# A fused recurrence and mixer kernel: SyncE's loads in another order, and the whole hand-held plan of engines, orders and banks replaced

## The chip, the cores and the metric

The kernel runs on one core of one Trainium2 chip. The core has a matrix engine (TensorE, PE in the profile; its weight loads are PEld), a vector engine (VectorE, DVE), a scalar engine with function tables (ScalarE, ACT), a general engine (GpSimd, POOL) and a queue engine (SyncE, SP) that here only issues transfers. Each engine takes its instructions strictly in the order in which the program gives them and waits on semaphores for results of the others. The metric is the time of one execution on the device in microseconds (us); lower is better. Several runs give a median.

## The reference: what is computed

Two stages follow each other, for batch B = 4, H = 8 heads, S = 768 tokens and D = 40 numbers per head (DM = H x D = 320). The first is a recurrence over tokens with a 40 x 40 state per batch and head:

```python
for t in range(S):
    y[:, :, t] = np.einsum('bhd,bhde->bhe', rt, state)
    Sa = np.einsum('bhde,bhe->bhd', state, at)
    state_decay = state * wt[:, :, None, :] - np.einsum('bhd,bhe->bhde', Sa, bt)
    state = state_decay + np.einsum('bhd,bhe->bhde', vt, kt)
```

The second is a mixer over the result x (heads laid side by side, 768 x 320 per batch), with two 768 x 768 matrices over tokens and two 320 x 320 matrices over channels:

```python
theta = x @ w_theta
zr, zi = x * cos(theta), x * sin(theta)
u = x + w_tok_r @ zr + w_tok_i @ zi
out = u + np.maximum(u @ w_ch, 0.0)
```

## The kernel before

**Tiles.** The recurrence is computed in chunks of 128 tokens: 6 chunks per batch, 24 tiles in all, numbered 0 to 23. Tile i needs six loads of 160 KB: w, k, b, a, v and r. For r, and for v of tiles 0 to 7 (called o there), two tiles are loaded together as two "runs" of 160 KB. The raw tiles stand in a few rotating buffers (`raw_w`, `raw_kb` four each, `raw_a` five, `raw_v` six halves, `raw_r` two pairs), so a load must also wait until the tile that had its buffer has been used up.

**Work of one tile**, by the names that the text uses (line numbers of the kernel before):

- ACT takes the logarithm of w (`lw`, L445). PE sums it along the tokens (`cs`, L458 to L464), ACT exponentiates the sums (`ex` L469, `we` L479 or L487).
- Products scale k, b and a (`kb`, `ah`; L428 on DVE or L429 on POOL). v and r are cast to bf16 (L434 on ACT, L435 on POOL).
- PE transposes kb, ah, v, r (L391, for runs L538, for the way back L557) into PSUM, and DVE (L397) or ACT (L394, for r L546) copies the result out. Such copies out of PSUM are called evacuations here.
- PE forms four score matrices of 128 x 1024 (L569): psi, phi, lamv and, later, lamu. Each must be masked to a triangle. There are two variants: DVE multiplies by a mask while it evacuates (L578), or ACT evacuates with a sign (L580) and POOL then clears one triangle in place (an affine select, L582; called a select below).
- PE then works through the state: `x0` (L610, L616), `nx` evacuated (L622 ACT, L623 DVE), `nu` (L629, evacuated at L633 or L635), the new state `gt` (L652, evacuated at L663 and L667, or L671) and its transpose `gd` (L679, evacuated at L684), the transposed nu (L391), scores lamu (`slu`), and the tile's result y (L793 to L802), which DVE multiplies out to x (L809).

**Mixer.** For two tiles at a time PE transposes x (L711), multiplies by w_theta (L763, L773), and ACT copies theta out (L828). After the last tile of a batch ACT takes sine and cosine (L850; these and the logarithm and exponential need different function tables, hence table loads at L850 and L1024). POOL or DVE forms zr and zi (L864, L865). For each of the six rows of tokens PE accumulates 12 matmuls of 320 columns (`row`, L881), DVE adds x (L887), PE transposes (L711) and multiplies by w_ch (L763, L773, L752), DVE adds the rectified product (L917, L905) and a transfer stores 160 KB (L920, L909). Late in the run eleven transposes go through the transfer engines instead (L698).

**What sets the order.** The kernel records 1,602 operations in a plan (`Plan`, L153), each with its engine, the data it reads and writes and its predecessors. Nothing is scheduled when the program is built: `Plan.order` (L186 to L199) takes the order from three tables that stand in the file.

- `ORDER` (L26) is a permutation of all operations. The program is emitted in it, and so it is each engine's own order and the order of SyncE's queue.
- `PICK` (L138) names the operations that use their other variant, that is the other engine. For a score, the mask on ACT and its select on POOL are two operations that are picked together.
- `HOMES` (L122) gives each PSUM result its bank, in order of its first use.

`WARM` (L145) adds 49 filler matmuls ahead of five early operations. The instructions of an engine are in-order, so an operation that waits holds up whatever stands behind it in `ORDER` on its engine.

The emission loop reads:

```python
for o in plan.order():
    ...
    if o.fn is not None:
        o.fn()
```

Of the kernel before, what the change touches and what calls it, by code (L numbers as in the profile page):

```python
# [26 lines left out]
    0, 7, 3, 6, 1, 2, 20, 8, 21, 23, 24, 4, 27, 9, 32, 30, 5, 22, 31, 33, 12, 25, 26, 34, 11,  # L27
    28, 10, 69, 35, 36, 29, 70, 37, 18, 47, 44, 40, 19, 48, 72, 45, 38, 41, 71, 49, 73, 39, 46,
    98, 119, 76, 99, 58, 14, 42, 100, 74, 57, 15, 13, 120, 122, 101, 50, 121, 79, 75, 51, 123,
    53, 106, 102, 107, 131, 108, 80, 52, 16, 77, 109, 132, 125, 78, 43, 103, 81, 17, 110, 134,  # L30
    126, 111, 133, 82, 56, 84, 137, 54, 104, 124, 138, 112, 129, 83, 85, 87, 130, 88, 127, 55,
    156, 86, 128, 59, 157, 89, 146, 184, 143, 90, 147, 105, 158, 61, 97, 60, 139, 187, 159,
    135, 62, 144, 148, 164, 96, 188, 160, 165, 191, 140, 93, 136, 145, 161, 166, 141, 91, 185,
    167, 213, 186, 92, 194, 214, 149, 189, 142, 162, 168, 150, 215, 163, 169, 190, 216, 195,
    152, 221, 170, 234, 151, 246, 192, 222, 235, 193, 237, 217, 95, 236, 202, 238, 218, 94,
    196, 203, 197, 63, 241, 155, 247, 171, 267, 248, 219, 239, 199, 198, 172, 220, 223, 205,
    249, 200, 240, 271, 64, 244, 272, 242, 299, 245, 201, 154, 273, 224, 243, 300, 173, 301,
    261, 206, 254, 274, 302, 225, 174, 262, 303, 279, 153, 175, 258, 306, 176, 255, 212, 259,
    263, 280, 250, 177, 204, 281, 256, 211, 275, 496, 282, 260, 320, 226, 251, 305, 257, 208,
    252, 276, 264, 283, 253, 317, 207, 227, 349, 327, 265, 277, 497, 328, 304, 309, 278, 329,  # L40
    498, 284, 266, 310, 270, 499, 330, 350, 285, 307, 351, 268, 318, 286, 354, 308, 269, 331,
    352, 500, 311, 361, 332, 319, 287, 314, 353, 312, 209, 336, 333, 539, 362, 210, 337, 289,
    356, 288, 315, 363, 313, 322, 290, 364, 338, 355, 291, 387, 325, 292, 339, 316, 365, 540,
    388, 359, 366, 389, 541, 357, 360, 340, 390, 341, 382, 358, 391, 321, 116, 503, 113, 501,
    542, 412, 373, 181, 342, 334, 376, 374, 502, 392, 367, 411, 326, 504, 377, 375, 506, 335,
    393, 368, 505, 323, 178, 369, 545, 524, 394, 378, 370, 507, 517, 525, 413, 508, 372, 526,
    384, 371, 509, 395, 416, 396, 527, 532, 417, 528, 397, 510, 511, 514, 529, 544, 117, 595,
    512, 572, 533, 415, 383, 530, 118, 398, 573, 515, 596, 513, 554, 385, 399, 534, 531, 574,
    418, 597, 401, 535, 400, 516, 575, 414, 402, 543, 379, 324, 404, 114, 567, 598, 536, 403,
    546, 548, 115, 380, 581, 642, 576, 582, 555, 601, 549, 577, 381, 583, 599, 66, 386, 550,  # L50
    584, 537, 557, 568, 600, 551, 182, 522, 558, 602, 183, 585, 586, 538, 619, 578, 561, 587,
    419, 179, 518, 559, 547, 604, 519, 556, 427, 180, 428, 421, 429, 605, 560, 420, 606, 520,
    423, 552, 607, 626, 553, 562, 434, 422, 627, 564, 435, 425, 436, 565, 563, 643, 628, 424,
    437, 644, 610, 566, 629, 426, 613, 645, 603, 588, 611, 630, 231, 523, 571, 521, 589, 438,
    430, 570, 698, 635, 631, 646, 612, 439, 431, 636, 632, 440, 608, 745, 432, 614, 699, 647,
    609, 746, 700, 675, 648, 747, 637, 433, 615, 676, 616, 701, 293, 569, 633, 677, 748, 634,
    651, 649, 638, 678, 590, 652, 684, 296, 579, 685, 679, 617, 639, 228, 620, 621, 580, 653,
    706, 657, 591, 654, 680, 592, 618, 686, 650, 593, 661, 703, 687, 594, 441, 622, 711, 702,
    640, 442, 681, 712, 662, 688, 655, 658, 705, 656, 689, 659, 641, 663, 660, 682, 704, 664,
    690, 749, 667, 683, 665, 691, 68, 709, 692, 707, 67, 710, 729, 668, 65, 670, 672, 666, 708,  # L60
    694, 693, 750, 624, 695, 730, 719, 713, 697, 751, 720, 731, 696, 232, 732, 294, 233, 297,
    714, 721, 295, 733, 738, 298, 229, 734, 739, 715, 716, 230, 740, 735, 717, 754, 450, 752,
    451, 778, 755, 718, 346, 625, 452, 779, 453, 741, 343, 623, 756, 881, 780, 454, 757, 408,
    882, 781, 742, 405, 673, 671, 764, 883, 767, 765, 669, 782, 884, 444, 722, 455, 783, 443,
    768, 456, 766, 445, 784, 446, 736, 457, 885, 785, 458, 760, 737, 743, 447, 459, 753, 448,
    786, 787, 887, 744, 761, 796, 788, 769, 758, 460, 759, 789, 763, 461, 888, 762, 790, 462,
    797, 912, 463, 792, 791, 913, 793, 723, 770, 795, 892, 771, 914, 794, 674, 893, 915, 886,
    772, 802, 890, 464, 891, 803, 773, 347, 465, 916, 348, 344, 799, 917, 905, 805, 409, 345,
# [988 lines left out]
```

## Time and profile before

| what | value |
|---|---|
| median of 3 runs | 199.94 us (199.28 to 202.03) |
| the profiled execution, its own time | 199.53 us |
| its span, first to last instruction | 197.8 us |
| PE busy | 187.6 us, 3288 matmuls |
| DVE, ACT, POOL busy | 164.3, 151.7, 145.1 us |
| loads by SyncE | 29.19 MB in its queue, 75.1% of the transfer engines' time |
| all transfers | 32.75 MB, 166 GB/s on average |
| operations on DVE, ACT, POOL after the set-up | 236, 327, 185 |

Busy times are sums of the durations of instructions. The ends of matmuls are modelled and consecutive ones overlap, so a PE that is "busy" may still start matmuls at less than its best pace. A line number such as L397 may be that of a helper which many operations share; the tile written and read tells them apart. In a view of waits, a row names the engine and line that waited, the engine and line that released it, the total in us, how often, and the longest.

### The profile page before, as it was taken

To read this page: it belongs to the slowest core of one execution; us is meant where nothing else is said; L and a number is where in the kernel's file an instruction comes from. 1 tells how busy PE (TensorE), PEld (TensorE's weight loads), DVE (VectorE), ACT (ScalarE), POOL (GpSimd) and SP (SyncE) were. 2 spreads that over 40 slices of the span, in tenths; PEclk is the share of its full clock that TensorE was granted. 3 is DMA by queue.
4 is the path that set the end of the run, shared out by engine and by line. 5 is a ranking of instruction groups with operands and counts; after the bars stand their busy time and mean duration, and the time that the engine had idled before them with its cause. 6 is when DMAs were issued, how large, how long until landed. Compare 5 with 4: busy or idle time off the path is not lost.

```text
span 197.8 us, 8019 instructions
## 1 busy us (share of the span) xinstructions
PE 187.6 (95%) x3288; PEld 150.3 (76%) x3288; DVE 164.3 (83%) x261; ACT 151.7 (77%) x337; POOL 145.1 (73%) x210
## 2 busy tenths in 40 slices
PE   7888999999989999999999999999999999999992
PEld 6776787777768788878878888888887878767661
DVE  5269899999989999888887988999999988675453
ACT  3584979799889988979988598888998986575111
POOL 8267544679879999699799939769699697558100
PEclk9999999999999999999999999999999999999999
DMA  6999879989999999999998899988998274863055
GB/s 119 210 212 163 154 161 196 182 166 197 233 174 173 207 171 185 190 185 223 153 210 168 153 187 170 188 148 169 182 155 163 43 177 102 87 194 104 0 191 174
DMA packets 134644, 32.75 MB, mean 166 GB/s; under 512 B 124816, under 2 KB 134608, under 8 KB 134608
## 3 DMA queue, kind: packets, MB, share of 16 engines
q1 hardware_dynamic: 131680, 29.19, 75.1%
q0 software_dynamic: 2784, 2.97, 9.6%
q8 instruction: 25, 0.41, 0.9%
q10 hardware_dynamic: 144, 0.08, 0.1%
q14 instruction: 11, 0.09, 0.1%
HBM read 29.54 MB, written 3.93 MB: 169 GB/s over the span
## 4 chain that ended last, share of the span: by engine, by line
PE 68%; DMA 9%; ACT 8%; SPq 6%; DVE 3%; issue 3%; POOL 1%; ACTq 0%; DVEq 0%; POOLq 0%
PE ps_s L881 17%; PE ps_s L391 10%; PE ps_d L569 9%; PE ps_s L763 5%; SPq L409 4%; DMA raw_w<-in_w_dram 3%; DMA raw_kb<-in_k_dram 3%; PE ps_s L711 3%; PE ps_s L652 2%; PE ps_s L629 2%; SPq L421 2%; DMA raw_r<-in_r_dram 2%; PE ps_s L538 2%; PE ps_s L773 2%; ACT cs L850 2%
## 5 line engine op out<-in xcount | busy, mean ns | idle before, releaser
L429 POOL TENSOR_TENSOR kb<-raw_kb,ex 128x320 bf16<-128x320 f32 x46 | 36.8, 811 | 9.7 <-DMA raw_kb<-in_k_dram 3.3
L881 PE MATMUL ps_s<-zr,wtok_r 128*128 128x320 bf16 x132 | 37.6, 299 | 0.0
L881 PE MATMUL ps_s<-zi,wtok_i 128*128 128x320 bf16 x132 | 37.5, 299 | 0.0
L578 DVE TENSOR_TENSOR lamu<-ps_d,mask_p 128x1024 bf16<-128x1024 f32 x22 | 26.8, 1219 | 1.7 <-PE ps_d L569 1.6
L578 DVE TENSOR_TENSOR psi<-ps_d,mask_p 128x1024 bf16<-128x1024 f32 x22 | 26.8, 1218 | 1.6 <-PE ps_d L569 1.4
L578 DVE TENSOR_TENSOR lamv<-ps_d,mask_p 128x1024 bf16<-128x1024 f32 x17 | 20.7, 1218 | 2.6 <-PE ps_d L569 1.8
L429 POOL TENSOR_TENSOR ah<-raw_a,we 128x320 bf16<-128x320 f32 x22 | 19.0, 866 | 3.6 <-DMA raw_a<-in_a_dram 1.6
L578 DVE TENSOR_TENSOR phi<-ps_d,mask_n 128x1024 bf16<-128x1024 f32 x17 | 20.7, 1218 | 0.9 <-PE ps_d L569 0.8
L865 POOL TENSOR_TENSOR zi<-cs,xp 128x320 bf16<-128x320 f32 x21 | 16.9, 816 | 3.3 <-ACT cs L850 3.3
L881 PEld LDWEIGHTS <-wtok_r 128*128 128x128 bf16 x144 | 14.0, 97 | 4.5
L569 PE MATMUL ps_d<-aT,kbT 64*128 64x128 bf16 x384 | 17.1, 217 | 0.2
L881 PEld LDWEIGHTS <-wtok_i 128*128 128x128 bf16 x144 | 14.1, 98 | 3.5
L391 PE MATMUL ps_s<-wide,kb 128*128 128x128 bf16 x184 | 15.0, 223 | 1.0 <-POOL kb L429 0.7
L865 POOL TENSOR_TENSOR zr<-cs,xp 128x320 bf16<-128x320 f32 x19 | 15.3, 810 | 0.7 <-ACT cs L850 0.7
L667 POOL TENSOR_TENSOR gt<-sum,ex 128x320 bf16<-128x320 f32 x13 | 9.5, 733 | 8.0 <-DVE sum L663 4.8
L800 PE MATMUL ps_s<-kb,lamv 128*128 128x40 bf16 x192 | 15.0, 180 | 0.0
L802 PE MATMUL ps_s<-kb,lamu 128*128 128x40 bf16 x192 | 14.9, 179 | 0.0
L569 PEld LDWEIGHTS <-kbT 64*128 64x128 bf16 x384 | 11.8, 94 | 3.1 <-ACT kbT L394 1.0
L800 PEld LDWEIGHTS <-lamv 128*128 128x128 bf16 x192 | 13.2, 96 | 0.6
L887 DVE TENSOR_TENSOR up<-ps_s,xp 128x320 bf16<-128x320 f32 x22 | 10.7, 488 | 3.5 <-PE ps_s L881 3.1
L435 POOL CAST r<-raw_r 128x640 bf16<-128x640 f32 x12 | 8.6, 720 | 6.5 <-DMA raw_r<-in_r_dram 6.5
L445 ACT ACTIVATE lw<-raw_w 128x320 bf16<-128x320 f32 x24 | 11.4, 475 | 2.6 <-DMA raw_w<-in_w_dram 2.6
(176 smaller groups left out, 606.7 us busy)
## 6 DMA issues: line engine op xcount, KB each, us to landing
raw_w<-in_w_dram SPq DMA_DIRECT2D x24, 160.0 KB, 4.1
raw_v<-in_v_dram SPq DMA_DIRECT2D x24, 160.0 KB, 3.9
raw_a<-in_a_dram SPq DMA_DIRECT2D x24, 160.0 KB, 4.2
raw_kb<-in_k_dram SPq DMA_DIRECT2D x24, 160.0 KB, 3.7
raw_kb<-in_b_dram SPq DMA_DIRECT2D x24, 160.0 KB, 4.0
raw_r<-in_r_dram SPq DMA_DIRECT2D x24, 160.0 KB, 4.4
out_dram<-oo SPq DMA_DIRECT2D x9, 160.0 KB, 2.0
wrow_i<-in_moe_w_tok_i_dram POOLq DMA_DIRECT2D x6, 192.0 KB, 5.3
```

What stands on the lines that cost most here:

```text
L391: nc.tensor.transpose(out=dst[:, c:c + 128], in_=pair(src, g), identity=ident)
L429: pool = ("POOL", lambda: nc.gpsimd.tensor_tensor(out=dst, in0=in0, in1=in1, op=ALU.mult))
L445: add("ACT", "ln", i, lambda: nc.scalar.activation(out=paired(lw)[:, :, :, 0:D], in_=paired(raw_w[s4]), func=AF.Ln), 473, [("raw_w", s4)], ...
L569: nc.tensor.matmul(t[:, q, g, :], lhsT=lhs[g][rows(q)], rhs=rhs[g][rows(q)], start=True, stop=True)
L578: add("DVE", kindm, i, lambda: nc.vector.tensor_tensor(out=flat, in0=whole(), in1=mask.to_broadcast([128, 2 * G, 128]), op=ALU.mult), 1217 ...
L667: add("POOL", "wgt", i, lambda: nc.gpsimd.tensor_tensor(out=new_state, in0=sum_t, in1=wm.to_broadcast([128, 8, D]), op=ALU.mult), 830, [(" ...
L763: nc.tensor.matmul(ps(pk)[:, 0:DM], lhsT=lhs[:, 3 * c + kt, :], rhs=wt[:, 3 * c + kt, :], start=kt == 0, stop=kt == 2, skip_group_check=n ...
L800: nc.tensor.matmul(o, lhsT=lamv[:, p, g, :], rhs=kb[:, 0, h, 0:D], start=first, stop=False, skip_group_check=True)
L802: nc.tensor.matmul(o, lhsT=lamu[:, p, g, :], rhs=kb[:, 1, h, 0:D], start=False, stop=True, skip_group_check=True)
L865: pool = ("POOL", lambda: nc.gpsimd.tensor_tensor(out=dst, in0=in0, in1=in1, op=ALU.mult))
L881: nc.tensor.matmul(acc(), lhsT=wtok[nm][j][:, s], rhs=zs[c][:, s], start=n == 0 and c == 0, stop=n == NT - 1 and c == 1)
L887: add("DVE", "uadd", q, lambda: nc.vector.tensor_tensor(out=u, in0=acc(), in1=x, op=ALU.add), 488, [pk, x_key(q)], [u_key(q)], at="row")
```

## The change

Nothing is computed otherwise. The program text is the same but for the three tables `ORDER`, `HOMES` and `PICK`; `WARM`, the crossbar transposes and the buffers are unchanged. The diff, cut to its core (two of some hundred lines of each list):

```diff
 ORDER = [
-    0, 7, 3, 6, 1, 2, 20, 8, 21, 23, 24, 4, 27, 9, 32, 30, 5, 22, 31, 33, 12, 25, 26, 34, 11,
-    28, 10, 69, 35, 36, 29, 70, 37, 18, 47, 44, 40, 19, 48, 72, 45, 38, 41, 71, 49, 73, 39, 46,
...
+    0, 1, 2, 3, 7, 20, 6, 21, 5, 23, 22, 24, 25, 26, 8, 27, 28, 12, 4, 30, 29, 10, 31, 32, 44,
+    9, 47, 45, 11, 33, 69, 70, 34, 35, 46, 119, 18, 48, 38, 71, 36, 122, 19, 58, 40, 120, 37,
...
 HOMES = [
-    4, 5, 5, 6, 5, 4, 7, 0, 2, 5, 4, 6, 7, 4, 5, 2, 7, 4, 5, 0, 4, 7, 2, 4, 0, 5, 6, 7, 2, 5,
...
+    4, 5, 4, 5, 0, 2, 7, 5, 7, 6, 4, 5, 6, 4, 7, 4, 5, 0, 5, 2, 6, 7, 4, 2, 0, 6, 5, 7, 4, 0,
...
 PICK = [
-    25, 31, 37, 39, 40, 48, 49, 75, 80, 85, 86, 115, 118, 130, 172, 180, 193, 203, 204, 222,
...
+    26, 35, 37, 64, 74, 76, 78, 85, 86, 88, 89, 99, 101, 107, 109, 110, 115, 118, 136, 138,
...
```

Translated into operations, this is what it does.

**SyncE's queue.** The first places, letter and tile (o and r: one run each):

```
before  w0 o0 a0 o0 k0 b0 w1 r0 k1 r0 w2 a1 b1 o2 o2 b2 a2 k2 w3 r2 r2 a3 k3 b3 w4 o4 o4 a4 k4 b4 w5 r4 r4 a5 w7 w6 b5 k6 k5 o6 o6
after   w0 k0 b0 a0 o0 o0 r0 w1 w2 r0 b1 k1 a1 o2 o2 b2 k2 w3 a2 w4 r2 r2 a3 k3 b3 o4 o4 a4 k4 b4 w5 r4 r4 k6 k5 a5 w7 w6 b5 o6 o6
```

Then both have w8 a6 b6; before goes on a7 k7 b7 r6 r6 b8 r8 w9 k8 r8 a8 w10 b9 k9 a9, after goes on b7 k7 a7 r6 r6 b8 w9 k8 r8 r8 a8 w10 b9 k9 a9. Of the later loads many move by two to ten places. After the last load, the stores of rows 3 and 4 stand ahead of the first crossbar transpose instead of behind the third, and some later stores change places.

**Engines.** 90 operations change their variant (a mask and its select counted apart):

| operations | moves |
|---|---|
| score masks | 9 from DVE to ACT, each with a new select on POOL (tiles 0, 1, 2, 2, 10, 10, 13, 18, 23); 2 from ACT to DVE, whose select goes (tiles 0, 13) |
| small evacuations and copies of 192 to 1024 numbers per partition | 33 from ACT to DVE, 17 from DVE to ACT |
| casts of r | 3 from POOL to ACT |
| casts of v | 4 from ACT to POOL, 1 from POOL to ACT |
| products kb, ah, z | 5 from POOL to DVE, 5 from DVE to POOL |

**Orders.** Each engine's order changes by a few places almost everywhere. In tile 0, PE transposes kb before ah, and both score groups stand ahead of the transposes of the o runs. At tile 4, one `gt` and one `slu` more stand ahead of the transpose of r (`tr`); at tile 6, `x0` stands behind it instead of ahead. On POOL the product for a of tile 2 stands behind two selects, and the casts of r and v of tile 12 behind two selects and a kb product. ACT changes its function table at the same nine places.

**Banks.** `HOMES` names a bank for each PSUM result anew, in the new order.

226 rows, old and new, of tables (HOMES, ORDER, PICK) are left out of this document.

## The prediction

> **What bounds the kernel now.** I read the page first, then two wide windows, then PE's waits, then the chain of waits. The page and the windows of the kernel before (columns: stretch, its length, busy us of PE, PEld, DVE, ACT, POOL, clock, DMA share, GB/s):
>
> ```profile
> span 197.8 us, 8019 instructions
> PE 187.6 (95%) x3288; PEld 150.3 (76%) x3288; DVE 164.3 (83%) x261; ACT 151.7 (77%) x337; POOL 145.1 (73%) x210
> ```
> ```profile
> 0.00:60.00 60.00, 54.13 (x993) 44.14 (x993) 49.43 (x85) 46.29 (x112) 40.72 (x72) 1.00 0.94 181
> 60.00:190.00 130.00, 129.46 (x2264) 103.83 (x2263) 111.19 (x169) 104.43 (x223) 104.37 (x139) 1.00 0.84 159
> ```
>
> PE is busy 54.13 of the first 60 us and 129.46 of the next 130: 5.87 us of visible idle before 60 us and 0.54 in all the rest. The ends of matmuls are modelled and their spans overlap, so short stalls can still hide in the second stretch. What PE waits for before 60 us (first fence), and the one wait of a compute engine for a load after 60 us (second; columns: us in total, times, longest):
>
> ```profile
> PE ps_s L1019 <- DVE busy L268: 1.1, 1, 1.1
> PE ps_s L711 <- ACT nuT L394: 0.9, 1, 0.9
> PE ps_s L391 <- POOL kb L429: 0.7, 3, 0.3
> PE ps_s L538 <- POOL r L435: 0.7, 2, 0.4
> PE ps_s L1019 <- ACT we L479: 0.5, 1, 0.5
> PE ps_s L629 <- ACT nx L622: 0.5, 1, 0.5
> PE ps_s L538 <- ACT o L434: 0.4, 1, 0.4
> PE ps_s L538 <- POOL o L435: 0.4, 1, 0.4
> ```
> ```profile
> POOL r L435 <- DMA raw_r<-in_r_dram: 0.5, 1, 0.5
> ```
>
> So there are two regimes. Up to 60 us landings pin the order: the chain of waits passes several times from SyncE's queue through a landing to one operand and on to PE:
>
> ```profile
> 13.29 5.87 DMA raw_kb<-in_k_dram
> ...
> 30.21 4.23 DMA raw_r<-in_r_dram
> 34.55 0.73 POOL r L435
> ...
> 48.11 6.82 DMA raw_w<-in_w_dram
> 54.95 0.03 ACT lw L445
> ```
>
> After 60 us the loads are early and PE's own work paces the rest. The change keeps PE's matmuls, their number and the 49 filler matmuls, so after 60 us only hidden short stalls can be won. Visibly, 0.9+0.7+0.7+0.5+0.5+0.4+0.4 = 4.1 us can be won before it (the first wait, 1.1, is the start).
>
> **The change part by part.** *Load order: the pins that stay.* While the queue is the bound, a place in it is a landing time. The loads that hold a pin keep their place: the o runs of tile 2, the whole a, k, b and r of tile 4, and r of tile 6. What is won ahead of one of these is waited off at it. Tile 0's k and b move from places 5 and 6 to 2 and 3, that is three places at the spacing of these issues
>
> ```profile
> 2.03 0.58 SPq L409 DMA_DIRECT2D raw_a<-in_a_dram  x1
> 2.65 0.59 SPq L421 DMA_DIRECT2D raw_v<-in_v_dram  x1
> ```
>
> of 0.62 us, so tile 0's scores come up to 1.9 us earlier; tile 2's o runs take that back. Tile 2's a moves two places back (1.2 us) and its product now stands on POOL behind two selects (1.1 us each, priced below): its own transpose and the scores behind it come up to 3.4 us later, which the pin at tile 4's r absorbs. At tile 4's r (lands at 30.21 + 4.23 = 34.44) the new order puts a gt and a slu more ahead of the waiting transpose, which fills up to 0.4 of PE's wait; at tile 6's r it puts x0 of tile 6 (0.35 us of matmuls) behind the transpose, so that these queue behind the same landing. Net 0 for all of it, bounds -0.5 and +0.5.
>
> *Load order: the pin that moves.* w of tile 9 changes places with an r run of tile 8:
>
> ```profile
> 46.44 1.57 SPq L421 DMA_DIRECT2D raw_r<-in_r_dram  x1
> 48.11 0.55 SPq L409 DMA_DIRECT2D raw_w<-in_w_dram  x1
> ```
>
> It is issued 1.67 us earlier. In both kernels ACT's next copy, which releases PE's transpose at L711, is queued behind the instruction that waits for it, and ACT has a table load ahead of both:
>
> ```profile
> 52.66 1.28 ACT L1024 ACT_TABLE_LOAD   x1
> 54.95 0.47 ACT L445 ACTIVATE lw<-raw_w 128x320 bf16<-128x320 f32 x1 [1.01 <-DMA raw_w<-in_w_dram]
> ```
>
> So ACT gains up to 1.01 and PE the 0.9 of its wait. I take -0.85; bounds 0 (it lands no earlier, since r's bytes were not what held it) and -1.0. What would be late next is k or a of tile 8, which keep their places.
>
> *Later loads.* After 60 us loads move by up to 10 places. POOL's whole wait on them there is the 0.5 above, so a and v of tile 15 and a of tile 18, three places later, are covered by that lead: 0, bounds 0 and +0.5. Two stores pass ahead of the first crossbar transpose, in a stretch where nothing is left to load: 0.
>
> *Engines.* Prices, from the groups by shape:
>
> ```profile
> L578 DVE TENSOR_TENSOR lamu<-ps_d,mask_p 128x1024 bf16<-128x1024 f32 x22 | 26.8, 1219 | 1.7 <-PE ps_d L569 1.6
> L580 ACT ACTIVATE phi<-ps_d 128x1024 bf16<-128x1024 f32 x7 | 7.2, 1031 | 0.5 <-PE ps_d L569 0.5
> L582 POOL TENSOR_SCALAR_AFFINE_SELECT phi<-phi 128x1024 bf16<-128x1024 bf16 x7 | 7.6, 1093 | 1.0 <-ACT phi L580 1.0
> L397 DVE COPY aT<-ps_s 128x512 bf16<-128x512 bf16 x8 | 3.4, 420 | 0.8 <-PE ps_s L391 0.7
> L435 POOL CAST r<-raw_r 128x640 bf16<-128x640 f32 x12 | 8.6, 720 | 6.5 <-DMA raw_r<-in_r_dram 6.5
> ```
>
> Nine score masks go from DVE to ACT with a select on POOL, two come back: DVE -7 x 1.22 = -8.5, ACT +7 x 1.03 = +7.2, POOL +7 x 1.09 = +7.7. Of the small evacuations 33 go to DVE and 17 leave it, at about 0.42 on either engine: DVE +6.7, ACT -6.7. Three r casts leave POOL for ACT (2.2); three v casts net go the other way (about half as long); a few products cancel. In all DVE about -2, ACT about +1, POOL about +7. DVE and ACT come out even. POOL has 60 - 40.7 = 19.3 us idle before 60 us and 130 - 104.4 = 25.6 after; three of its seven selects (net) fall in tiles 0 to 2, where it waits for loads anyway. The exception is tile 10, which gets two where POOL is full and its casts feed PE at once:
>
> ```profile
> 70.00:80.00 10.00, 10.00 (x215) 8.53 (x213) 9.88 (x14) 8.89 (x25) 9.98 (x16) 1.00 1.16 189
> 80.00:90.00 10.00, 10.00 (x190) 8.11 (x188) 8.60 (x12) 8.42 (x20) 8.39 (x12) 1.00 1.07 185
> ```
> ```profile
> 89.53 0.74 POOL L435 CAST r<-raw_r 128x640 bf16<-128x640 f32 x1
> ```
> ```profile
> 90.90 0.61 PE L538 MATMUL ps_s<-wide,r 128*128 128x128 bf16 x8
> ```
>
> Two selects are 2.2 us against 1.6 of idle, so 0.6 late; tile 12's r cast, done at 90.27, has 0.6 in hand before PE takes it. It also moves behind a kb product. I take +0.3, between 0 and +2.2.
>
> *Tail.* The same last operations in nearly the same order; tile 22's row sum ends a little closer to its transpose. +0.1, bounds 0 and +0.3.
>
> **Sum**: -0.85 + 0.3 + 0.1 = -0.45. The profiled execution took 199.53 (the span of 197.8 and 1.7 around it), so 199.1. The median of the runs, 199.94, lies 0.4 above that execution and within their spread (199.28 to 202.03); I add nothing for it.
>
> **The clock, where row and rule meet.** The first 25 filler matmuls stand 114 ns apart, the eleven from 11.34 us on 55 ns apart (until the next group at 11.95):
>
> ```profile
> 1.13 2.85 PE L1019 MATMUL ps_s<-busy 128*128 128x128 bf16 x25 [1.13 <-DVE busy L268]
> ...
> 11.34 0.78 PE L1019 MATMUL ps_s<-busy 128*128 128x128 bf16 x11
> 11.95 0.61 PE L538 MATMUL ps_s<-wide,r 128*128 128x128 bf16 x8
> ```
>
> PE starts at half pace and has its full pace by 11.3 us, though the granted clock reads 1.00 throughout. The new order spaces PE's first groups differently; if the full pace came one filler stretch (2.85 us) later, the matmuls in that stretch would take up to 1.4 us more. The Trainium skill (TensorE: Matmul & The Clock Gate, "What's actually happening") states that the gate opens after a window of about 3.4 us in which PE was busy; the doubling in the rows agrees, and one more such window at half pace would be an estimate of 1.7 us, a sum of 200.8.
>
> **The rivals.** *POOL becomes the bound (slower).* A select waits on POOL's in-order queue for ACT's mask; the 18 selects cost 1.4 + 1.3 + 1.3 + 1.0 = 5.0 us of such idle, 0.28 each:
>
> ```profile
> POOL lamu L582 <- ACT lamu L580: 1.4, 1, 1.4
> POOL psi L582 <- ACT psi L580: 1.3, 1, 1.3
> POOL lamv L582 <- ACT lamv L580: 1.3, 1, 1.3
> POOL phi L582 <- ACT phi L580: 1.0, 2, 0.6
> ```
>
> The two of tile 10 and one each of tiles 18 and 23 would then hold up the casts and products behind them for 4 x 1.37 = 5.5 us: 199.4 + 5.5 = 204.9. It decides once tile 12's casts end after PE is ready for them; the idle counted above speaks against it. *All visible early waits go (faster).* 199.5 - 4.1 = 195.4; the pins that keep their places speak against it. *Nothing ends differently.* w of tile 9 comes early, but another operand of tile 8 or 9 is late in its stead: 199.5 + 0.4 = 199.9. *Half pace lasts longer*: 199.1 + 1.4 = 200.5.
>
> **How the numbers follow.** Forecast 0.50 (199.1; its own range 198.0 to 200.2), nothing different 0.22, half pace 0.08, POOL 0.12, early waits gone 0.08. About 2% (4 us) is what a measurement of this kernel can tell from no change: faster by more 0.08, slower by more 0.12, within 0.80. The bounds of the terms add up to 199.5 - 1.5 = 198.0 and 199.5 + 3.5 = 203.0. The range leaves out the two outer cases: down to 196.7, halfway to the faster one, and up to 203.0.
>
> **What would show it.** Right: PE busy over 129 of the 130 us after 60 us; its wait at L711 gone before 60 us, ACT's lw starting near 54; tile 0's scores near 9 us, but tile 4's r cast still near 34.5. Wrong: PE waiting over 1 us on POOL between 78 and 98 us, or visible PE idle before 60 us under 4 or over 7 us.

## The result, and the profile after

The changed kernel takes 202.25 us (median of 19 runs, 200.84 to 205.87), the kernel before on the same chip 201.14 (19 runs, 198.32 to 204.35). The ratio is 1.0108 with a 95% interval of 1.0082 to 1.0135: 1.6 to 2.7 us slower, 2.2 at the middle. The ratio compares only executions within 1.5% of their kernel's fastest, which leaves out eight of the 19 before and two of the 19 changed; the medians of all lie 1.1 us apart. The forecast was 199.1, that is 0.4 faster than its profiled execution. The time lies in the range and within 2%, but the sign is wrong.

The page of the changed kernel, then its two wide windows (columns as before: stretch, length, PE, PEld, DVE, ACT, POOL busy, clock, DMA share, GB/s):

```profile
span 200.5 us, 8008 instructions
PE 187.3 (93%) x3288; PEld 150.2 (75%) x3288; DVE 162.5 (81%) x270; ACT 153.2 (76%) x328; POOL 152.5 (76%) x217
```
```profile
0.00:60.00 60.00, 53.85 (x991) 44.46 (x991) 47.67 (x86) 47.26 (x111) 44.67 (x77) 1.00 0.95 181
60.00:190.00 130.00, 127.55 (x2249) 101.88 (x2246) 109.91 (x174) 104.50 (x215) 107.81 (x141) 1.00 0.84 158
```

The profiled execution took 202.2 us beside 199.53, its span is 2.7 us longer. PE's work is the same. Before 60 us its visible idle is 6.15 (5.87 before). After 60 us PE is busy 127.55 of 130, where it was 129.46: the stretch that had 0.54 us of visible idle has 2.45. PE's waits in this stretch (total, times, longest) name four places, none of which stood there before:

```profile
PE ps_s L765 <- DMA xT<-xp: 0.9, 1, 0.9
PE ps_d L571 <- ACT vT L396: 0.6, 1, 0.6
PE ps_s L393 <- POOL kb L431: 0.5, 1, 0.5
PE ps_s L618 <- POOL psi L584: 0.4, 1, 0.4
```

(Lines are two higher than in the kernel before, for the lengthened tables.) Each leads to a transfer.

*vT.* ACT's rows of the changed kernel (start, duration, instruction, idle ahead of it), and those of the kernel before:

```profile
70.14 0.47 ACT L447 ACTIVATE lw<-raw_w 128x320 bf16<-128x320 f32 x1 [0.99 <-DMA raw_w<-in_w_dram]
70.52 0.35 ACT L396 COPY vT<-ps_s 128x256 f32<-128x256 f32 x1
```
```profile
69.72 0.47 ACT L445 ACTIVATE lw<-raw_w 128x320 bf16<-128x320 f32 x1
70.21 0.37 ACT L394 COPY vT<-ps_s 128x256 f32<-128x256 f32 x1
```

The copy of tile 9's vT stands behind tile 12's logarithm in both, but now the logarithm waits 0.99 us for its w, which the queue issues two places later. Two places are not the whole delay: the issue directly ahead of it, b of tile 10, took 1.71 us, and w went out 2.83 us later. SyncE's rows, changed kernel (b of tile 10, w of tile 12) and kernel before (w of tile 12):

```profile
63.99 1.71 SPq L411 DMA_DIRECT2D raw_kb<-in_b_dram  x1
65.80 0.58 SPq L411 DMA_DIRECT2D raw_w<-in_w_dram  x1
```
```profile
62.97 0.55 SPq L409 DMA_DIRECT2D raw_w<-in_w_dram  x1
```

In the kernel before this w landed 3.40 us after its issue, at 66.37, and so 3.35 us ahead of its logarithm. In the changed kernel it landed after 4.25 us, at 70.06. The later issue and the longer landing use up a lead that was there.

*kb and psi.* In the chain of waits b of tile 11 lands 7.45 us after its issue; POOL's product waits 1.2 us for it, and a select of tile 10, new on POOL, is queued behind. The chain (start, duration, piece), then POOL's wait:

```profile
70.76 7.45 DMA raw_kb<-in_b_dram
...
78.27 1.14 POOL kb L431 x2
...
79.79 1.10 POOL psi L584
```
```profile
POOL kb L431 <- DMA raw_kb<-in_b_dram: 1.2, 1, 1.2
```

*xT.* SyncE's issues late in the run, changed kernel first:

```profile
167.52 1.23 SPq L700 DMA_TRANSPOSE uT<-up  x1
168.85 0.53 SPq L922 DMA_DIRECT2D out_dram<-wrow_i  x1
169.47 1.19 SPq L700 DMA_TRANSPOSE nuT<-nu  x1
170.75 1.23 SPq L700 DMA_TRANSPOSE xT<-xp  x1
172.07 2.38 SPq L700 DMA_TRANSPOSE uT<-up  x1
```
```profile
166.57 1.23 SPq L698 DMA_TRANSPOSE uT<-up  x1
167.89 1.22 SPq L698 DMA_TRANSPOSE nuT<-nu  x1
169.21 1.24 SPq L698 DMA_TRANSPOSE xT<-xp  x1
170.54 2.39 SPq L698 DMA_TRANSPOSE uT<-up  x1
173.02 0.53 SPq L920 DMA_DIRECT2D out_dram<-wrow_i  x1
```

A store, that of row 6, now stands among the crossbar transposes instead of behind them, and PE waits 0.9 us for xT of tile 20.

The signs named ahead of the run were mixed. The wait at the old L711 is gone. Tile 9's lw starts at 54.77 and waits for nothing. Tile 0's scores come at 8.55 (10.41 before). But tile 4's r cast is not near 34.5, and PE takes its result only much later (POOL's row, then PE's):

```profile
32.93 0.72 POOL L437 CAST r<-raw_r 128x640 bf16<-128x640 f32 x1
```
```profile
37.83 0.56 PE L540 MATMUL ps_s<-wide,r 128*128 128x128 bf16 x7
```

So a landing no longer pins PE there: PE is late by itself. Between 20 and 40 us POOL waited 6.6 us for loads in the kernel before; in the changed one it waits for none, but 5.4 us for ACT's exponentials (`ex`).

**A ruler for all executions.** A wait of one execution need not be in the next. What can be compared are distances between fixed matmuls. I use four points: the first x0 matmul of tile 4, of tile 8 and of tile 10, and the first nu matmul of tile 22; then the end of PE's last matmul, and the end of the span. For the two kernels (us, each start read off the timeline):

| | x0 tile 4 at | x0 tile 8 at | 8 to 10 | 10 to nu 22 | nu 22 to PE's end | end of span |
|---|---|---|---|---|---|---|
| before | 38.34 | 64.82 | 14.54 | 86.72 | 28.24 | +3.49 |
| changed | 39.79 | 64.41 | 15.94 | 86.60 | 29.27 | +4.25 |
| difference | +1.45 | -0.41 | +1.40 | -0.12 | +1.03 | +0.76 |

The last five differences add up to the 2.7 us between the spans. In this pair the late start is made up by 64 us, and the time is lost between tiles 8 and 10 and in the last 30 us.

### The profile page after: what moved, and what is told of

Read it like the earlier page. It is cut to its first block, busy times and chain, and to the rows that moved or that the text cites. A ratio compares the mean times of both kernels' runs of the same rounds, so it can differ in the third digit from the quotient of the medians.

```text
span 200.5 us, 8008 instructions
## 1 busy us (share of the span) xinstructions
PE 187.3 (93%) x3288; PEld 150.2 (75%) x3288; DVE 162.5 (81%) x270; ACT 153.2 (76%) x328; POOL 152.5 (76%) x217
## 4 chain that ended last, share of the span: by engine, by line
PE 68%; DMA 8%; ACT 8%; POOL 6%; DVE 3%; issue 3%; SPq 2%; DVEq 0%; POOLq 0%; ACTq 0%
PE ps_s L883 16%; PE ps_d L571 10%; PE ps_s L393 9%; PE ps_s L765 5%; DMA raw_kb<-in_b_dram 4%; PE ps_s L540 3%; PE ps_s L713 2%; PE ps_s L631 2%; DMA xT<-xp 2%; PE ps_s L654 2%; PE ps_s L775 2%; PE ps_s L618 2%; PE ps_s L804 2%; PE ps_s L802 2%; DMA raw_w<-in_w_dram 1%
## 5 line engine op out<-in xcount | busy, mean ns | idle before, releaser
L580 DVE TENSOR_TENSOR psi<-ps_d,mask_p 128x1024 bf16<-128x1024 f32 x21 | 25.6, 1218 | 2.5 <-PE ps_d L571 2.4
L580 DVE TENSOR_TENSOR lamu<-ps_d,mask_p 128x1024 bf16<-128x1024 f32 x21 | 25.6, 1218 | 0.8 <-PE ps_d L571 0.7
L431 POOL TENSOR_TENSOR ah<-raw_a,we 128x320 bf16<-128x320 f32 x23 | 19.9, 865 | 1.7 <-ACT uT L396 0.9
L580 DVE TENSOR_TENSOR phi<-ps_d,mask_n 128x1024 bf16<-128x1024 f32 x16 | 19.5, 1217 | 0.1
L867 POOL TENSOR_TENSOR zi<-cs,xp 128x320 bf16<-128x320 f32 x20 | 16.4, 832 | 2.4 <-ACT cs L852 2.4
L580 DVE TENSOR_TENSOR lamv<-ps_d,mask_p 128x1024 bf16<-128x1024 f32 x13 | 15.8, 1216 | 1.2 <-PE ps_d L571 1.2
L571 PEld LDWEIGHTS <-kbT 64*128 64x128 bf16 x384 | 12.4, 95 | 4.4 <-issue 2.3
L393 PE MATMUL ps_s<-wide,kb 128*128 128x128 bf16 x184 | 14.5, 223 | 0.5 <-POOL kb L431 0.5
L471 ACT ACTIVATE ex<-ps_s 128x328 f32<-128x328 f32 (+1 forms) x24 | 10.8, 450 | 4.3 <-PE ps_s L466 2.2
L584 POOL TENSOR_SCALAR_AFFINE_SELECT lamv<-lamv 128x1024 bf16<-128x1024 bf16 x11 | 12.0, 1092 | 2.1 <-ACT lamv L582 2.1
```

The costliest lines, as they stand in the source:

```text
L393: nc.tensor.transpose(out=dst[:, c:c + 128], in_=pair(src, g), identity=ident)
L431: pool = ("POOL", lambda: nc.gpsimd.tensor_tensor(out=dst, in0=in0, in1=in1, op=ALU.mult))
L471: got = add("ACT", "exp", i, lambda: nc.scalar.activation(out=ex[:, :, 0:D] if no_total else ex.rearrange("p h x -> p (h x)"), in_=sums(ps ...
L571: nc.tensor.matmul(t[:, q, g, :], lhsT=lhs[g][rows(q)], rhs=rhs[g][rows(q)], start=True, stop=True)
L580: add("DVE", kindm, i, lambda: nc.vector.tensor_tensor(out=flat, in0=whole(), in1=mask.to_broadcast([128, 2 * G, 128]), op=ALU.mult), 1217 ...
L584: add(None, "sel", i, None, 0, [dkey], [dkey], alts=(("POOL", lambda: nc.gpsimd.affine_select(out=flat, in_=flat, pattern=[[0, 2 * G], [1, ...
```

## The experiments

Theory 1: the loss is in the late part, where loads, transposes and stores stand at other places in SyncE's queue than the work needs. Rival 2: the new start (39.79 instead of 38.34 at tile 4) is what is paid, and the later waits only show it. Rival 3: the new engine orders themselves, whatever lands when. Rival 4: half pace of PE at the start.

Most kernels join the two plans. At the places 308, 429, 891 and 1360 of `ORDER` (about 43, 58, 109 and 160 us) both plans have done the same operations but for at most one, which goes where its predecessors allow. Each operation keeps the variant and bank of the plan from which it comes (a few banks are given anew where they would still be in use). `b` and `a` in the diffs are the `ORDER` of before and of after. Each time stands against the kernel before on the same chip: the ratio, its 95% interval, and the ratio as us of that chip's median. The diffs are put in short.

### The late part, the middle and the step at 43 to 58 us

```diff
+ORDER = b[:1360] + a[1360:]              # late_only
+ORDER = b[:429] + a[429:891] + b[891:]   # mid_only
+ORDER = b[:308] + a[308:429] + b[429:]   # w9_only
```

> The kernel before up to 160 us, and from there the changed kernel's orders, engines and banks (the two plans have done the same set of operations at that point, so the cut is clean). Theory A, that part of the loss is the crossbar transpose for tiles 20 and 21 landing late at 175 us: the time is 0.7 to 1.3 us over before, and PE's wait for xT from the transfer, 0.9 us in the changed kernel, is there again. Rival B, that the late orders are covered and all of the loss comes from earlier: within 0.3 us of before, no such wait.

> The kernel before, but with the changed kernel's plan from 58 to 109 us (loads of tiles 10 to 15, the two selects of tile 10, POOL's order there). Theory A, that the rest of the loss is b of tile 11 landing late and the select of tile 10 queued behind the product that waits for it: 0.7 to 1.5 us over before, a POOL wait for b of some 1.2 us and PE waits of some 0.5 us for kb and for psi near 80 us. Rival B, that tile 10's place is a lag carried in from the first 58 us: within 0.3 us of before.

> The kernel before, but with the changed kernel's plan from 43 to 58 us, which has w of tile 9 one place earlier and one engine choice changed. Theory A, that this step was priced rightly and its gain was eaten by the late head: 0.6 to 1.0 us under before, ACT's lw of tile 9 near 54 us, the 0.9 us wait of PE for the transpose at the end of tile 5 gone. Rival B, that another operand is late in its stead: within 0.3 us of before.

late_only: 1.0066 (1.0033 to 1.0099), +1.3 us. mid_only: 1.0049 (1.0016 to 1.0083), +1.0 us. w9_only: 1.0006 (0.9981 to 1.0031), +0.1 us.

The end alone is slower by 0.7 to 2.0 us, so part of the loss is there and needs no new start. In PE's waits of late_only between 160 and 190 us there is one row, at the matmuls that take xT:

```profile
PE ps_s L767 <- DVE up L891: 0.7, 1, 0.7
```

The DVE operation that it names ended at 172.59, in the same moment in which the crossbar transpose landed; the matmuls, which start at 172.63, read xT and not `up`, so I count this as the transpose.

The times of mid_only are slower by 0.3 to 1.7 us, but its profiled execution does not show why: neither the wait for b of tile 11 nor PE's waits for kb and psi are there, and PE's only wait there, 1.1 us for a product of a, ends at 59.96.

w9_only removes the wait at the old L711 and gains nothing. Its PE waits between 40 and 66 us tell why:

```profile
PE ps_d L573 <- DVE phi L582: 0.5, 1, 0.5
PE ps_s L797 <- DVE kbT L401: 0.4, 1, 0.4
PE ps_d L573 <- ACT nuT L398: 0.3, 1, 0.3
PE ps_s L542 <- ACT nuT L398: 0.2, 1, 0.2
```

They sum to 1.4 us. In the same stretch the kernel before has the 0.9 at L711 and two waits of 0.3, in all 1.5. One wait was exchanged for four small ones.

### The start: loads, engines, both

```diff
+ORDER = a[:308] + b[308:]                       # head_only
+ORDER = b, the loads within b[:300] in a's order   # head_loads
+ORDER = a[:300], its loads in b's order, + b[300:] # head_engines
+ORDER = a[:429] + b[429:]                       # head58
```

> The changed kernel's plan up to 43 us (some 1.4 to 1.7 us behind the kernel before at that point, as its trace has it), then the plan of before. Theory A, that the head is late and the wait for w of tile 9 near 55 us absorbs what is late up to about its own 0.9 us: 0.3 to 0.9 us over before. Rival B, that the landings at tile 6 and tile 9 absorb it all: within 0.3 us of before. Rival C, that nothing absorbs it: 1.4 to 1.7 us over before.

> The kernel before with one thing changed: SyncE's first loads (those of the first 42 us) stand in the changed kernel's order; no engine's order and no variant is touched. Theory A, that the late head comes from the loads (the o runs of tile 0 behind k, b and a; r and k of tile 1 behind two more w): 1.4 to 2.3 us over before, with PE's lag there by tile 1. Rival B, that it comes from the engines' orders and variants in tiles 0 to 3: within 0.4 us of before, since the landings of tiles 2 to 6 stay where they were.

> The reverse: the changed kernel's orders, variants and banks up to 42 us, but SyncE's loads there in the order of the kernel before, and the plan of before after that. Theory A (loads): within 0.5 us of before. Rival B (engines): 1.4 to 2.3 us over before, like the changed head as a whole (which came to 2.3 with an interval of 1.4 to 3.2). If each alone costs 1 us or more, it is the order that no longer fits its landings, whichever is changed.

> The changed kernel's plan up to 58 us, then the plan of before: the late head with the new place of w of tile 9 and of POOL's products of tile 8. Theory A, that the new order from 43 to 58 us takes back about 1 us of the late head, by putting sine products where POOL had waited for k of tile 8: 0.7 to 1.5 us over before. Rival B, that nothing is taken back: 2 us or more over before. What is left to the changed kernel's 2.2 us is then the price of everything after 58 us.

head_only: 1.0115 (1.0072 to 1.0159), +2.3 us. head_loads: 1.0048 (1.0019 to 1.0078), +1.0. head_engines: 1.0181 (1.0134 to 1.0227), +3.6. head58: 1.0038 (1.0004 to 1.0073), +0.8 (0.1 to 1.5).

The new start costs by itself. The engine orders are the larger part: they cost 3.6 with the old loads and 1.3 on top of the new ones (2.3 beside 1.0). The new loads cost 1.0 under the old orders and gain 1.3 under the new ones: loads and orders of the start belong together. With the changed plan up to 58 us most of it is recovered, but not all: 0.1 to 1.5 us are left.

### One store moved back

```diff
-... store of row 6, transposes of nu, x and u ...
+... transposes of nu, x and u, store of row 6 ...
```

> The changed kernel with one store (row 6) moved back behind the crossbar transposes of nu of tile 22, x of tiles 20 and 21 and u of rows 12 to 15, where the kernel before had it. Theory A, that this store's 0.6 us in the queue makes x of tile 20 land late at 175 us: PE's wait for it falls from 0.9 to 0.3 us or less, and the time is 0.6 us under the changed kernel, 1.4 to 1.8 us over before. Rival B, that the queue is late for another reason (its transposes' own issue times): the wait stays at 0.7 us or more.

1.0073 (1.0035 to 1.0112), +1.5 us, where the changed kernel had +2.2. SyncE's rows, and no wait of PE between 160 and 190 us is left:

```profile
167.73 1.23 SPq L704 DMA_TRANSPOSE uT<-up  x1
169.05 1.22 SPq L704 DMA_TRANSPOSE nuT<-nu  x1
170.36 1.23 SPq L704 DMA_TRANSPOSE xT<-xp  x1
171.69 1.23 SPq L704 DMA_TRANSPOSE uT<-up  x1
173.01 1.66 SPq L926 DMA_DIRECT2D out_dram<-wrow_i  x1
```

From nu of tile 22 to PE's end this kernel, and each of the three others with the same end, takes 27.93 us. The five executions with the changed end and whole loads take 28.83 to 29.37, 29.10 on average. So this one store costs 1.17 us of PE's time. The two times differ by 0.7 with overlapping intervals; the distances are the firmer evidence.

### The rest after 58 us, and the part from 109 to 160 us

```diff
+ORDER = b[:429] + a[429:]                # rest58
+ORDER = b[:891] + a[891:1360] + b[1360:] # d_only, d_again
```

> The kernel before up to 58 us and the changed kernel's plan after it. The changed plan up to 58 us alone came to 0.8 us over before (0.1 to 1.5), the whole change to 2.2 (1.6 to 2.7). Theory A, that the two parts add up: 0.9 to 1.9 us over before, with PE's wait for x of tile 20 from the transfer near 175 us. Rival B, that the rest only costs what it does behind the late head: within 0.5 us of before.

> The kernel before with the changed kernel's plan from 109 to 160 us only. In the changed kernel's trace PE falls less behind there than in the kernel before: 0.4 to 0.8 us are won back between 123 and 137 us. Theory A, that this part of the change is a gain: 0.4 to 0.9 us under before. Rival B, that it is chance of one execution: within 0.3 us of before.

> d_only once more. Theory A, that the gain is real: 0.4 to 2 us under before again. Rival B, that it was chance: within 0.4 us of before.

rest58: 1.0057 (1.0000 to 1.0113), +1.1 us. d_only: 0.9942 (0.9902 to 0.9982), -1.2 us. d_again, the same kernel run once more later: 1.0019 (0.9980 to 1.0058), +0.4 us.

The gain of d_only did not repeat, so nothing is built on it. In rest58 tiles 8 to 10 take 14.76, not 15.94: the loss there does not come with the changed order alone. mid_only, which like rest58 has the old plan from 43 to 58 us, takes 14.75; in both, w of tile 12 lands 0.5 us ahead of its logarithm, and the issue of b of tile 10 takes 0.67 and 0.96 us. In the four executions with the changed plan on both sides of 58 us and its own loads the issue takes 1.71 to 2.23 us, w is late and the tiles take 15.67 to 16.36. What holds that issue up is not settled. The parts up to 58 us (head58, +0.8) and after it (rest58, +1.1) add up to 1.9. In d_again the wait of the old L711 is even longer than in the kernel before, though its code is the same up to 109 us (PE's waits before 60 us):

```profile
PE ps_s L715 <- ACT nuT L398: 1.5, 1, 1.5
```

### Loads of 58 to 80 us back

```diff
 # the changed plan; SyncE's loads within places 429 to 620:
-... in a's order ...
+... in b's order ...
```

> The changed kernel with SyncE's loads issued from about 54 to 80 us (k of tile 9 to v of tile 12) back in the order of the kernel before; w of tile 12 stands there two places earlier. No engine's order and no variant is touched. Theory A, that in this stretch a load's place costs, since ACT's logarithm of w of tile 12 waits for its landing with the copy of v of tile 9 behind it (PE waits of 0.6 and 1.0 us in two executions): that wait is gone and the time is 0.4 to 1.0 us under the changed kernel, 1.2 to 1.8 us over before. Rival B, that after 58 us loads are early whatever their order: as the changed kernel, 2.2 us over before.

1.0085 (1.0045 to 1.0125), +1.7 us. Tile 12's w is no longer waited for, yet tiles 8 to 10 take 16.27. Now v of tile 11 is late on POOL:

```profile
74.83 0.45 POOL L441 CAST v<-raw_v 128x320 bf16<-128x320 f32 x1 [0.96 <-DMA raw_v<-in_v_dram]
```

The simple reading, that w's place in the queue is the fault, falls. Moving one load back makes another late for the new engine order.

### Half of each load left out

```diff
+    def part(i):
+        return 128 if i < 6 else 64
...
-                lambda dst=dst, src=src: nc.sync.dma_start(out=dst, in_=src),
+                lambda dst=dst[0:part(i)], src=src[0:part(i)]: nc.sync.dma_start(out=dst, in_=src),
```

From tile 6 on, the second half of each tile's partitions is not loaded and keeps what an earlier tile left there; the runs of o and r are cut alike.

> The kernel before, with each load from tile 6 on cut to the first 64 of its 128 partitions (the other half keeps what an earlier tile left there; all instructions of PE, DVE, ACT and POOL stay). Theory A, that the stream of loads stands close behind its use up to 147 us: 0.5 to 2 us under before, without the PE waits for kb, ah and the copies behind lw of tiles 8 and 9 near 55 to 60 us. Rival B, that the loads are early anyway after 60 us: within 0.5 us of before.

> The changed kernel with its loads cut in the same way. Theory A, that beside the store of row 6 (0.7 to 1.2 us) and the late head (some 0.8 us) the changed plan loses only at landings: no wait for w of tile 12 or b of tile 11, PE's lag to the kernel before with such loads does not grow between 64 and 165 us, and the whole is 1.2 to 2.0 us over half_before. Rival B, that its orders cost by themselves between 58 and 109 us as well: 2.2 us or more over half_before, with PE waits there as in the changed kernel.

half_before: 0.9871 (0.9816 to 0.9925), 197.79 us. half_after: 0.9973 (0.9938 to 1.0008), 199.95 us. The windows after 60 us, half_before and then half_after:

```profile
60.00:190.00 130.00, 129.46 (x2237) 103.60 (x2235) 110.90 (x170) 103.01 (x220) 101.68 (x135) 1.00 0.56 100
```
```profile
60.00:190.00 130.00, 129.31 (x2277) 103.77 (x2276) 111.19 (x176) 105.14 (x217) 108.11 (x142) 1.00 0.56 102
```

With the DMA share at 0.56 instead of 0.84, the idle after 60 us is gone in the changed kernel too (127.55 before the cut, 129.31 now), and tiles 8 to 10 take 14.62 us: that loss is one of landings. But the difference of the two medians is still 2.2 us. It now comes from the start, since little takes it up again: x0 of tile 4 stands at 37.83 and 40.10 (+2.27), that of tile 8 at 62.95 and 64.72 (+1.77); then +0.08, -0.79, +0.62 and, behind PE's end, +0.7.

### The fillers ahead of the first scores left out

```diff
-WARM = {21: 25, 30: 4, 33: 1, 28: 8, 41: 11}
+WARM = {21: 25, 30: 4, 33: 1, 28: 8, 41: 0}
```

> The changed kernel without the eleven filler matmuls ahead of r's transpose of tile 0, which now stand between x0 and nu of tile 0 (0.6 us of PE), where in the kernel before they lay in a wait for r. Theory A, that they are part of the late head: PE comes to nu of tile 0 about 0.6 us earlier, and the time is 0 to 0.6 us under the changed kernel. Rival B, that the clock falls to half pace without them, since PE then idles: PE is later at tile 1 than in the changed kernel, and the time 0.5 us or more over it.

1.0140 (1.0087 to 1.0193), +2.8 us. The profiled execution of the changed kernel still ran PE at half pace at 8.55 us, that of no_fill did not (eight fillers and the first score matmuls; changed, then no_fill):

```profile
5.32 1.01 PE L1021 MATMUL ps_s<-busy 128*128 128x128 bf16 x8 [0.24 <-ACT ex L471]
...
8.55 1.04 PE L571 MATMUL ps_d<-aT,kbT 64*128 64x128 bf16 x16 [0.46 <-ACT aT L396]
```
```profile
5.25 0.61 PE L1021 MATMUL ps_s<-busy 128*128 128x128 bf16 x8 [0.36 <-ACT ex L471]
...
7.94 0.62 PE L571 MATMUL ps_d<-aT,kbT 64*128 64x128 bf16 x16 [0.49 <-ACT aT L396]
```

The eight fillers stand ahead of what was left out, so the pace there is the execution's own and not the edit's. In no_fill nu of tile 0 came at 13.99 instead of 14.62, but the eleven fillers that are missing there took 0.61 us; head58, at full pace and with them, has 14.29. x0 of tile 4 stands at 39.59, as late as in the changed kernel (39.79). Of the six executions with the changed start and its loads, four ran these eight fillers at full pace (head_only, head58, st6_back, no_fill) and reach tile 4 at 39.31 to 41.51; the two at half pace (changed, loads58_back) reach it at 39.79 and 39.14. Half pace does not explain the late start.

### Joining the better parts

```diff
+ORDER = b[:308] + a[308:429] + b[429:891] + a[891:]   # best1
+ORDER = b[:891] + a[891:]                             # best2
+ORDER = b[:308] + a[308:]                             # repaired
 # in all three the store of row 6 stands behind the transposes
```

> The parts that did no harm alone, together: the kernel before up to 43 us and from 58 to 109 us, the changed kernel's plan from 43 to 58 us and from 109 us to the end, with the store of row 6 moved back behind the crossbar transposes. Theory A, that the parts add: 0.1 to 0 for the first, 0.4 to 0.9 won by the second, 0.2 won at the end (PE's wait for x of tile 20 gone): 0.4 to 1.2 us under before. Rival B, that landings of loads set the time whatever the later plan does: within 0.3 us of before.

> The kernel before up to 109 us, then the changed kernel's plan to the end, with the store of row 6 back behind the crossbar transposes. Theory A, that the gain of the stretch from 109 to 160 us (1.2 us, interval 0.4 to 2.0) and the earlier crossbar transposes (PE 0.2 us less behind over the last stretch than in the kernel before) add: 0.8 to 1.6 us under before. Rival B, that the gain was chance of those runs: within 0.4 us of before.

> The changed kernel with both named causes undone: up to 43 us the plan of the kernel before, and the store of row 6 back behind the crossbar transposes. Theory A, that these two are the loss: within 0.6 us of before on either side, some 2 us under the changed kernel. Rival B, that PE, once it is earlier, only meets the landings of tiles 11 and 12 instead: 1 us or more over before, with PE waits between 68 and 82 us.

best1: 0.9966 (0.9921 to 1.0012), -0.7 us. best2: 1.0016 (0.9972 to 1.0060), +0.3. repaired: 1.0075 (1.0039 to 1.0110), +1.5. No join is reliably faster than the kernel before. repaired has the start of the kernel before and the mended end, and still loses 0.8 to 2.2 us, so these two are not the whole loss; tiles 8 to 10 take 15.95, and the same wait is there as in the changed kernel:

```profile
71.32 0.47 ACT L450 ACTIVATE lw<-raw_w 128x320 bf16<-128x320 f32 x1 [1.68 <-DMA raw_w<-in_w_dram]
71.69 0.35 ACT L399 COPY vT<-ps_s 128x256 f32<-128x256 f32 x1
```

### All executions beside each other

The points of the ruler, read off each profiled execution. The letters tell the plan of the five parts (to 43, 58, 109, 160 us, and the end): b before, c changed, s changed with the store moved back.

```
                    x0_4   x0_8   8->10  10->nu22  nu22->end
before       bbbbb  38.34  64.82  14.54  86.72     28.24
w9_only      bcbbb  37.38  63.50  14.55  86.74     28.16
late_only    bbbbc  37.59  63.71  14.54  86.70     28.83
mid_only     bbcbb  38.06  64.23  14.75  86.30     28.13
d_only       bbbcb  38.03  65.11  14.54  86.82     28.13
d_again      bbbcb  37.96  66.16  14.54  86.68     28.13
rest58       bbccc  37.77  66.00  14.76  86.39     29.37
best1        bcbcs  38.43  64.54  14.54  86.81     27.93
best2        bbbcs  37.54  64.57  14.54  87.12     27.93
repaired     bcccs  38.17  64.90  15.95  86.20     27.93
head_loads   loads  39.51  64.61  14.54  87.67     28.13
head_engines orders 41.60  67.49  14.54  87.40     28.25
head_only    cbbbb  39.51  66.01  14.55  86.47     28.13
head58       ccbbb  39.31  64.69  14.54  87.93     28.15
changed      ccccc  39.79  64.41  15.94  86.60     29.27
st6_back     ccccs  41.51  66.13  15.67  85.91     27.93
no_fill      ccccc  39.59  65.37  16.36  86.34     28.93
loads58_back ccccc  39.14  64.60  16.27  86.58     29.12
half_before  bbbbb  37.83  62.95  14.54  86.71     28.13
half_after   ccccc  40.10  64.72  14.62  85.92     28.75
```

From it, with whole loads:

- **To tile 4:** 37.4 to 38.4 with the old start, 39.1 to 41.5 with the new one. The ranges do not meet; the means of the ten rows that begin with b (37.93) and the six that begin with c (39.81) differ by 1.9 us.
- **To tile 8:** the seven rows with bb average 64.94, the five with cc 65.04, the three with bc 64.31 and the one with cb 66.01. The rows scatter by 2.5, but most of the 1.9 is no longer there: I take +0.1, though the 0.8 by which head58's time is longer is within this scatter too.
- **Tiles 8 to 10:** 14.54 or 14.55 in all twelve rows with the old plan there (half_before among them), 14.75 to 16.36 with the changed one. The six with its own loads fall into two groups: 14.75 and 14.76 with the old plan from 43 to 58 us (mid_only, rest58), and 15.67 to 16.36 with the changed one, 15.98 on average, +1.44. In these four (changed, st6_back, no_fill, repaired) PE's wait is for ACT's vT behind tile 12's lw: 0.6, 1.0, 1.4 and 1.3.
- **Tile 10 to nu of 22:** the five rows with the changed plan and its own loads average 0.8 less than the seven with the old one (86.29 and 87.09), but 0.4 less when the three old rows are left out that wait on POOL for b of tile 21 (head_loads, head_engines, head58). d_only, d_again and best2 show no gain. I count it as not settled.
- **The end:** +0.94 on average, of which the store is 1.17.
- **Behind PE's end** (not in the table): 3.49 to 3.61 us with the old end. With the changed order of the last stores it is 3.67 in late_only, 3.78 in best1, best2 and repaired, and 4.11 to 4.34 in the others, so it is not the order alone; for the changed kernel I take +0.6.

0.1 + 1.44 - 0.8 + 0.94 + 0.6 = 2.3, or 2.7 with the -0.4, beside the 1.6 to 2.7 measured; the sum is no sharper than that. The theory stands in its main point (the larger part of the loss is after 60 us, in the queue's order against the work), but not in its simple form: an order of loads is good or bad only with the engine orders that it serves. Rival 2 is not refuted: with whole loads the plan up to 58 us alone costs 0.1 to 1.5 us by the times, and with halved ones the start is most of the difference. Rival 3 holds for the start, where +1.9 and +2.27 appear at tile 4 with whole and halved loads. Rival 4 falls.

## Why the prediction was wrong, step by step

- **w of tile 9, -0.85: failed.** The mechanism was right: the wait is gone in each execution with the changed plan there and present in five of seven with the old code up to 58 us. But alone it costs +0.1 (-0.4 to +0.6) us; by the ruler the three bc rows are at tile 8 0.6 ahead of the seven with bb, within the scatter. The step that failed is "ACT gains up to 1.01 and PE the 0.9 of its wait": what came next was not late in landing but not ready, masks and copies on DVE and ACT (the four waits of w9_only, 1.4 us in all). This is the rival "nothing ends differently", true for this term.
- **The head, net 0: near the sum by the ruler (+0.1), above it by the time of head58 (+0.8), and the reason is wrong.** "The pin at tile 4's r absorbs" fails. r's cast went at 32.93 and PE came for it at 37.83. At tile 4 the changed start is 1.9 us behind, outside the bounds of 0.5. Most of it is taken up later, with the new order from 43 to 58 us (head_only +2.3, head58 +0.8) and while loads still land late (with halved loads 1.77 of 2.27 are left at tile 8).
- **Later loads, 0 to +0.5: failed, +1.44 in the four executions like the changed kernel.** The failing step is "POOL's whole wait on them there is the 0.5 above": one engine's wait in one execution was taken for the slack of all, and the moves of other loads got no term. w of tile 12 had no row in the waits, since it had 3.35 us of lead; two places later, behind an issue of 1.71 us and with a landing longer by 0.85, nothing of it was left. In the changed kernel's own execution b of tile 11 is late as well (PE's waits for kb and psi, 0.9).
- **Tile 10's selects, +0.3 (0 to 2.2): too large.** The work moved as forecast (busy DVE -1.8, ACT +1.5, POOL +7.4 us; forecast -2, +1, +7), but it cost nothing there. With halved loads tiles 8 to 10 cost 0.08, and the stretch behind them, in which tile 12's cast lies, is shorter by 0.79. PE's waits on POOL there sum to 0.9, under the 1 us named, and only where a late b stands ahead of the select. The rival "POOL becomes the bound" falls with it: in half_after POOL is busy 108.11 us and PE still 129.31. (Its 204.9 starts from 199.4; the other terms, -0.85 and +0.1, give 198.8, so 204.3.)
- **Stores, 0: failed, and this is the most directly shown.** The two stores that the text named (rows 3 and 4) were priced at nothing "in a stretch where nothing is left to load"; no stretch of the ruler shows a cost of these two. But what stands behind a store there is a transpose, not a load. The store that costs 1.17 us, row 6, was in the list of changes ("some later stores change places") and got no term at all.
- **The tail, +0.1 (0 to 0.3): mis-sized, +0.6, cause open.** The text looked at the last operations on PE, and not at the queue behind them. SyncE's last issues, changed and before:

```profile
193.47 0.81 SPq L922 DMA_DIRECT2D out_dram<-oo  x2
194.33 0.45 SPq L922 DMA_DIRECT2D out_dram<-wrow_i  x1
...
196.85 0.40 SPq L922 DMA_DIRECT2D out_dram<-o  x1
```
```profile
191.17 0.33 SPq L920 DMA_DIRECT2D out_dram<-oo  x1
191.55 0.42 SPq L920 DMA_DIRECT2D out_dram<-wrow_r  x1
...
194.87 0.33 SPq L920 DMA_DIRECT2D out_dram<-o  x1
```

  Eight stores go out back to back from 193.47 in the changed kernel, where the store of row 19 stands ahead of those of rows 18, 17 and 16. This order explains only a part: late_only, best1, best2 and repaired have it too and end 3.67 to 3.78 us behind PE. The last store goes out 0.62 us behind PE's end (0.55 before), but lands 2.47 us after its issue instead of 1.79, and why is not known.
- **Half pace, a rival:** it did occur in the profiled execution, but it occurs in some executions of a plan and not in others, and at tile 4 no cost of it is seen.

The forecast and the changed kernel's profiled execution lie 3.1 us apart (199.1 and 202.2). By the stretches of the ruler in this pair: to tile 8, -0.85 was forecast and -0.41 came (0.4); tiles 8 to 10, 0 and +1.40 (1.4); then, where tile 12's cast lies, +0.3 and -0.12 (-0.4); the end, 0 and +1.03 (1.0); behind it, +0.1 and +0.76 (0.7).

## What to carry to other kernels

When a plan is replaced, price every moved transfer by what stands behind it in its own queue, stores among transposes above all, and each engine's load-fed instruction by its lead over the landing, not by whether the profile shows a wait. A lead counts only as far as the issues ahead of the transfer keep their pace. An order of loads and the engine orders that use it are one thing: the old loads under the new orders were worse at the start (3.6 beside 2.3) and not clearly better after 58 us (1.7 beside 2.2). Where runs scatter by 2 us, compare distances between fixed matmuls over many executions; one stretch repeated to 0.01 us in twelve of them, and so showed a loss that the times alone could not place.

## What the runs showed of the hardware

- **Pace of PE at the start.** With the granted clock at 1.00, the same eight fillers took 1.01 us from 5.32 in the changed kernel and 0.61 from 5.25 in no_fill, whose program is the same up to there; the changed kernel's scores at 8.55 still go at half pace. The Trainium skill (TensorE: Matmul & The Clock Gate, "What's actually happening") says that the gate's window runs freely, so that the change to full pace varies by about 0.5 us. The rows agree that it varies, but these two executions differ by more than 3 us; PE was not busy without a break in either (it waits 0.24 and 0.36 us just ahead of these fillers).
- **Crossbar transposes in SyncE's queue.** They go out about 1.3 us apart (some 2.4), and a store between two of them takes 0.62 more, from 168.85 to 169.47. x of tile 20, issued at 170.75, landed 4.28 us later.
- **Landings scatter.** Among the seven rows that share program and load order up to 58 us, w of tile 9 landed 6.64 to 8.46 us after its issue, and the start of tile 8's x0 differs by up to 2.5 us between executions. From there to tile 10, PE's distance with the old plan repeats to 0.01 us.
